# Block-sparse attention into a Sinkhorn mixture of experts: a planned end at the last adding DMA, a later planned landing of the first values, and a new table of priorities

## The chip, the cores and the metric

The kernel runs on one core of one Trainium2 chip. The metric is the time of one execution in device microseconds (us). TensorE (PE) multiplies, VectorE (DVE) and ScalarE (ACT) read its results out of PSUM and work elementwise, GpSimd (POOL) and SyncE (SP) mostly issue DMAs, as ScalarE does now and then. Each of these engines takes its own instructions strictly in the order in which the program holds them: an instruction that waits holds up all that stand behind it on its engine.

## The reference

q, k and v have the shape (4, 8, 768, 64): 4 batches, 8 heads, 768 positions. Attention looks at a band of near positions and at 24 block summaries (the maximum of the keys, the mean of the values of 32 positions each):

```python
k_sum = k.reshape(B, H, nb, block, D).max(axis=3)        # block = 32
v_sum = v.reshape(B, H, nb, block, D).mean(axis=3)
mask_l = np.abs(pos[:, None] - pos[None, :]) < window    # window = 16
scores_all = np.concatenate([scores_l_m, scores_s], axis=-1)   # scores_s has + log(32)
...                                                      # softmax -> a
attn = np.matmul(a, np.concatenate([v, v_sum], axis=2))
```

Its result, as x of 3072 rows and 512 columns, goes through 8 experts, whose weights per row come from 8 Sinkhorn steps:

```python
P = np.exp(x @ w_gate - max)                 # 3072 x 8
for _ in range(8):
    P /= P.sum(1, keepdims=True) + 1e-09
    P /= P.sum(0, keepdims=True) + 1e-09
    P *= N / E
for e in range(E):
    out += P[:, e:e + 1] * (np.maximum(x @ w1[e], 0.0) @ w2[e])   # w1[e]: 512 x 1024, w2[e]: 1024 x 512
```

## The kernel before, in words

**The planner.** The order of the instructions is made when the program is built, by the class `Plan` (lines 39 to 130), a list scheduler. The kernel hands it units: each has an engine (or a choice between two) with a planned cost in us, units that it depends on, a priority (the smaller number first), PSUM banks that it opens or uses, and a `lag`, the planned time from its end until those that depend on it may start. `order()` lays the units out in planned time, and the functions of the units are called in that order, which thereby becomes the order of each engine's queue. At each step it takes, engine by engine, the unit that can start first; among those that can start within 0.02 us of each other the priority decides. A unit without a function (`fn` is None) issues nothing. Such units stand on names that are no engines, `"LAND"` above all: they only tell the plan when a transfer has landed. The waits that the hardware performs come from what the instructions read and write, not from the plan. Where the plan sees TensorE idle during the first stage, `plan.idle` puts in filler matmuls on zeros (line 597).

**The attention stage.** The 32 heads go in 16 pairs (`i`), four to a batch. GpSimd issues the loads of q, k and v, which also convert the type. For each pair TensorE transposes k and q (`tkq`), ScalarE or VectorE copies them out as kT and qT, TensorE makes the scores of the band (`sg`) and of the summaries (`ss`), ScalarE the exponentials, and TensorE multiplies with the values. `block_sums(i)` (line 398) are six matmuls that sum the values of each block (`vs`); they read v as loaded (`vx`) and depend in the plan on the unit `U["v", i]`. `block_out(i)` (from line 402) scales them into `V_s` on VectorE. For pair 0, k and q come in through separate loads in halves; `load_pair(0, "v")` puts the load of v into the plan and sets `U["v", 0]` to its landing. The pairs of batch 0 are worked on in halves of 384 rows, and expert 0 (`hidden0`, `hps` at line 226; `project0`, `yps` at line 236) runs between the pairs as soon as its rows of x are there. For the later batches `near_values` brings the neighbours' values in place through SyncE's queue, and some of k is transposed by DMA (`kT<-kst`).

**Experts 1 to 7.** Each product is a Strassen-Winograd scheme. The rows go in 3 blocks `j` (`NJ`), each in 2 halves `u`: 42 half blocks (`duos`). `plan_duo` plans the first product of one (line 991: `pab`, `pg`; and 1049, 1377), whose results ScalarE copies (`c`, line 1115) and VectorE joins (line 941), with the relu at line 217; VectorE forms the sums of the left-hand sides (`hf`, line 935). `plan_pair` plans the second product of four quarters `c` of each block as seven products `q1` to `q7` (lines 997 and 1377: `px`, `py`); `plan_twin` has one more level for most blocks. For experts from 2 on, ScalarE and VectorE scale the results by P into parts in `out_acc` (`e0` to `e4`: lines 1265, 1246), and GpSimd adds them to `out` in HBM by accumulating DMAs, `da` (line 1286) and `db` (line 1289). `da` needs `e0` and `e3`, and `e3` reads the product `q3`. In the plan the two cost GpSimd 1.0 us each, and the unit `d["landed"]`, which comes 4.0 us later, tells that they have landed.

The last block (expert 7, `j` = 2) goes another way: SyncE fetches the rows as summed so far from HBM (`fetch`), VectorE adds the last products to them (`t0` to `t4`, lines 1231 and 1246), and plain stores (line 1238) on SyncE's queue, two on ScalarE's, write the final rows. So the last adding DMAs are those of the block before it (expert 7, `j` = 1), and no unit of the plan depends on their landing.

**Priorities.** `feed(n)` plans half block n: its first product together with the second product of half block n - 2. `base` is 10000 + 100 n, and each unit's priority is `base` plus a number out of the table `PR` (by `rank`: one for the name, one more for the name in its block), or in the last block one number `name.l<c>` for each quarter:

```python
def rank(name, k):
    return PR[name] + PR.get(f"{name}.{k}", 0.0)
```

The numbers run to several thousand, so they reach far beyond the 100 by which one half block follows the other.

Of the kernel before, what the change touches and what calls it, by code (L numbers as in the profile page):

```python
# [140 lines left out]
def kernel(  # L141
# [12 lines left out]
    B, H, S, D = q.shape  # L154
    G = S // 128
    N, DM = out.shape
    E = moe_w_gate.shape[1]
# [85 lines left out]
    NS = 1  # L243
# [9 lines left out]
    if True:  # L253
# [19 lines left out]
        add = plan.add  # L273
# [574 lines left out]
        load_pair(0, "v")  # L848
        load_pair(1, "k0")
# [70 lines left out]
    if True:  # L920
# [639 lines left out]
        for u in course:  # L1560
# [266 lines left out]
        def feed(n):  # L1827
# [47 lines left out]
            if n < len(duos):  # L1875
# [3 lines left out]
                if e >= 2 and (n == 8 or e > 2 and (j, u) == (0, 0)):  # L1879
                    w2_sub_sums(e, base + PR["NW"], [pairs[1, NJ - 1, 3]["landed"]] if n == 8 else [])  # L1880
# [49 lines left out]
```

## Time and profile before

| | |
|---|---|
| median of 3 runs | 665.35 us (665.2 to 665.42) |
| the profiled execution | 667.84 us |
| its span, first to last instruction | 665.8 us |
| mean granted TensorE clock | 0.993 of full |
| HBM read, written | 55.59 MB, 45.09 MB |

The span is what the trace covers; the time of the execution also holds what lies around it. The second part of the page cuts the span into 40 slices of 16.6 us: each digit is the busy share in tenths (9 is 90% or more), PEclk the granted TensorE clock in tenths of full speed. The fifth groups the instructions: line, engine, operation, output and input, number; then busy time, mean ns of one, and the idle time in front of them with what ended most of it.

```profile
PE   8999999999999999999999999999999999999994
DVE  6879898678899979896799779868888788977874
ACT  5776766555996678898898999988999888998861
POOL 8699504222102022434244243524352436533321
PEclk8999999999999999999999999999999999999998
...
L1286 POOL DMA_DIRECT2D out_dram<-out_acc x68 | 63.9, 940 | 87.4 <-ACT out_acc L1265 47.4
...
L1115 ACT COPY c<-pab 128x512 f32<-128x512 f32 x84 | 50.1, 597 | 15.8 <-PE pab L991 11.5
```

The slices show where TensorE isn't full: the first and the last one. GpSimd issues 68 adding DMAs at line 1286, each of which occupies it for some 0.94 us. The copies at line 1115, one kind of ScalarE's work in the expert stage, take 0.6 us each.

In the views of waits, `<-` names what ended a wait. In a timeline a row begins with its start and its length in us, both for the run of instructions that `x` counts; a number in square brackets is the wait just ahead. The rows that name an engine with a q (SPq, POOLq, ACTq) are the engines' own queue work: DMA issues, semaphores and drains.

### The profile page before, as it was taken

The numbers are of one execution on the slowest core, as the hardware profiler recorded it, in microseconds if no ns is written. First come the engines' busy times: TensorE is split into PE (matmuls) and PEld (weight loads), VectorE is DVE, ScalarE is ACT, GpSimd is POOL, SyncE is SP. The second block draws the span as 40 slices with busy tenths as digits, with TensorE's granted clock in tenths as the row PEclk, the third lists the DMA queues.
The fourth block names the chain that finished last, engine by engine and source line by source line (L and its number), as shares of the span: only waits on it lengthen the run. The fifth ranks groups of instructions, "written<-read, shape, count | busy, mean of one in ns | idle before, by whom it ended". The sixth has DMA issues, their size and how long they took to land.

```text
span 665.8 us, 15109 instructions
## 1 busy us (share of the span) xinstructions
PE 651.5 (98%) x5575; PEld 447.4 (67%) x5575; DVE 545.8 (82%) x1356; ACT 528.7 (79%) x1183; POOL 258.9 (39%) x320
## 2 busy tenths in 40 slices
PE   8999999999999999999999999999999999999994
PEld 4666665555667766676776767767677676776773
DVE  6879898678899979896799779868888788977874
ACT  5776766555996678898898999988999888998861
POOL 8699504222102022434244243524352436533321
PEclk8999999999999999999999999999999999999998
DMA  9999976800727257977989599969997899979576
GB/s 161 184 150 147 132 92 66 103 1 1 142 79 129 96 122 109 115 101 100 170 97 140 69 152 130 110 99 125 139 108 96 115 162 134 148 95 208 88 96 159
DMA packets 147369, 77.75 MB, mean 117 GB/s; under 512 B 112736, under 2 KB 125280, under 8 KB 147296
## 3 DMA queue, kind: packets, MB, share of 16 engines
q0 software_dynamic: 124864, 62.64, 80.7%
q1 hardware_dynamic: 21472, 13.68, 8.3%
q8 instruction: 44, 0.72, 0.4%
q10 hardware_dynamic: 960, 0.48, 0.2%
q14 instruction: 29, 0.24, 0.1%
HBM read 55.59 MB, written 45.09 MB: 151 GB/s over the span
## 4 chain that ended last, share of the span: by engine, by line
PE 82%; DVE 7%; issue 6%; DMA 2%; POOL 2%; POOLq 0%; ACT 0%; DVEq 0%
PE pab L991 16%; PE pg L991 15%; PE py L997 14%; PE px L997 12%; PE px L1377 7%; PE yps L236 5%; PE hps L226 5%; PE pab L1049 4%; DVE xs L552 1%; DMA kT<-kst 1%; DMA vx<-in_v_dram 1%; PE sg L388 1%; POOL out_dram L1289 1%; POOL out_dram L1286 1%; PE tkq L354 1%
## 5 line engine op out<-in xcount | busy, mean ns | idle before, releaser
L997 PEld LDWEIGHTS <-hf 128*128 128x128 f16 x1840 | 179.0, 98 | 50.3
L1289 POOL DMA_DIRECT2D out_dram<-out_acc x68 | 63.8, 938 | 150.9 <-ACT out_acc L1265 88.8
L1286 POOL DMA_DIRECT2D out_dram<-out_acc x68 | 63.9, 940 | 87.4 <-ACT out_acc L1265 47.4
L935 DVE TENSOR_TENSOR hf<-hf 128x1024 f16<-128x1024 f16 x142 | 94.5, 688 | 2.5
L997 PE MATMUL py<-w,hf 128*128 128x256 f16 x656 | 93.8, 273 | 0.0
L941 DVE CUSTOM_DVE_ANT_0 hf<-pg,c 128x512 f16<-128x512 f32 x84 | 57.6, 686 | 30.6 <-ACT c L1115 18.6
L1265 ACT ACTIVATE out_acc<-py,P_sb 128x256 f32<-128x256 f32 x136 | 64.9, 489 | 10.3 <-PE py L997 6.8
L991 PEld LDWEIGHTS <-ws 128*128 128x128 f16 x504 | 47.8, 98 | 30.3 <-issue 0.2
L941 DVE CUSTOM_DVE_ANT_0 hf<-pab,c 128x512 f16<-128x512 f32 x84 | 57.7, 687 | 10.3 <-PE pab L991 4.5
L202 POOL DMA_DIRECT2D w<-in_moe_w_dram x56 | 46.2, 903 | 50.7 <-PE pg L991 44.1
L991 PEld LDWEIGHTS <-w 128*128 128x128 f16 x520 | 48.3, 98 | 24.0 <-issue 0.2
L1115 ACT COPY c<-pab 128x512 f32<-128x512 f32 x84 | 50.1, 597 | 15.8 <-PE pab L991 11.5
L217 ACT ACTIVATE hf<-pg 128x512 f16<-128x512 f32 x84 | 50.4, 601 | 12.0 <-PE pg L991 11.8
L997 PE MATMUL px<-ws,hf 128*128 128x256 f16 x400 | 59.8, 273 | 0.0
L997 PE MATMUL px<-w,hf 128*128 128x256 f16 x400 | 58.5, 273 | 0.0
L991 PE MATMUL pab<-xT,w 128*128 128x512 f16 x184 | 53.9, 379 | 0.0
L1107 ACT COPY pg<-pab 128x512 f32<-128x512 f32 x84 | 49.8, 594 | 3.7 <-PE pab L1049 3.6
L217 ACT ACTIVATE hf<-pab 128x512 f16<-128x512 f32 x84 | 51.1, 615 | 1.5 <-PE pab L991 0.9
L1122 ACT COPY c<-pg 128x512 f32<-128x512 f32 x84 | 49.7, 592 | 1.4 <-PE pg L991 0.8
L991 PE MATMUL pg<-xTs,w 128*128 128x512 f16 x168 | 50.0, 379 | 0.0
L991 PE MATMUL pg<-xTs,ws 128*128 128x512 f16 x168 | 50.0, 379 | 0.0
L991 PE MATMUL pg<-xT,w 128*128 128x512 f16 x168 | 50.0, 379 | 0.0
(190 smaller groups left out, 1513.6 us busy)
## 6 DMA issues: line engine op xcount, KB each, us to landing
out_dram<-out_acc POOLq DMA_DIRECT2D x136, 256.0 KB, 5.2
w<-in_moe_w_dram POOLq DMA_DIRECT2D x8, 1024.0 KB, 11.3
w<-in_moe_w_dram POOLq DMA_DIRECT2D x56, 128.0 KB, 4.9
out_dram<-out_acc SPq DMA_DIRECT2D x28, 256.0 KB, 2.1
vx<-in_v_dram POOLq DMA_DIRECT2D x16, 192.0 KB, 6.0
qst<-in_q_dram POOLq DMA_DIRECT2D x31, 96.0 KB, 5.5
kst<-in_k_dram POOLq DMA_DIRECT2D x24, 96.0 KB, 5.2
out_acc<-out_dram SPq DMA_DIRECT2D x8, 256.0 KB, 5.0
```

Of the source, the lines that this page charges most:

```text
L217: nc.scalar.activation(out=out, in_=in_, func=AF.Relu, bias=0.0, scale=1.0)
L935: nc.vector.tensor_tensor(out=out, in0=in0, in1=in1, op=ALU.subtract)
L941: nc.vector._custom_dve(TENSOR_ADD_SAT, out=out, in0=in0, in1=in1, s0=FLT_MAX, s1=0.0)
L991: nc.tensor.matmul(bank[:], lhsT=w[:, dk, :], rhs=x[:, dk, :], start=start and dk == 0, stop=dk == KH - 1, skip_group_check=True)
L997: nc.tensor.matmul(bank, lhsT=a(f)[:, 128 * c:128 * (c + 1)], rhs=w[:, f, :], start=start and f == 0, stop=f == FH - 1, skip_group_check=True)
L1107: nc.scalar.copy(out=B["g" + K][:], in_=B["a" + K][:])
L1115: nc.scalar.copy(out=B["c5" + K][:], in_=B["b" + K][:])
L1122: nc.scalar.copy(out=B["c2" + K][:], in_=B["g" + K][:])
L1265: nc.scalar.activation(out=out_acc[:, (c, HT + c)[t == tb], k * DH:(k + 1) * DH], in_=at(src), func=AF.Copy, scale=scale[:, t, e:e + 1])
L1286: nc.gpsimd.dma_start(out=rows(ta), in_=out_acc[:, c, :], accum_op=ALU.add)
L1289: nc.gpsimd.dma_start(out=rows(tb), in_=out_acc[:, HT + c, :], accum_op=ALU.add)
L1377: nc.tensor.matmul(half(b, k)[:, g, :], lhsT=still2(e, j, g, w, c)[:, i, :], rhs=moving2a(e, g, v)[:, i, :], start=start and g == 0 and i ...
```

## The change

Three edits. First, behind the load of pair 0's values, a unit that issues nothing moves `U["v", 0]` by 1.6 us in the plan; `block_sums(0)` is planned from there:

```diff
         load_pair(0, "v")
+        U["v", 0] = add("LAND", 0, None, [U["v", 0]], lag=1.6)
         load_pair(1, "k0")
```

Second, in `feed`, once the last half block is planned, a unit `END` that issues nothing depends on the landing of the last adding DMAs:

```diff
+            if n == len(duos) + 1:
+                put("END", 0, None, [pairs[E - 1, NJ - 2, c]["landed"] for c in range(4)], 0)
             m = n - 2
```

Third, the numbers of the table `PR` are replaced; its names stay. A few of them, among them those of the last block's `q3` and `t0` to `t4`:

```diff
         PR = {
-            "m1": 2584.1, "m5": 3374.6, "m2": -1146.9, "m6": -1658.9, "m3": -213.8, "m7": 4417.6,
+            "m1": 2568.5, "m5": 1010.4, "m2": -2957.6, "m6": -785.6, "m3": 391.2, "m7": 2631.7,
...
-            "Nn5": 302.7, "Nnh": -1488.9, "Nn2": 1284.0, "Nn6": -1478.7, "Nj1": -592.1, "Nn3": -840.8,
+            "Nn5": -2485.2, "Nnh": 1513.2, "Nn2": -262.5, "Nn6": -1417.6, "Nj1": 1456.6, "Nn3": -646.5,
...
-            "q7.l2": -1606.8, "q7.l3": -662.9, "q3.l0": 3956.3, "q3.l1": -2000.3, "q3.l2": 6715.0, "q3.l3": 1656.4,
+            "q7.l2": 712.5, "q7.l3": 357.8, "q3.l0": 308.9, "q3.l1": 1053.1, "q3.l2": -1088.2, "q3.l3": 2816.7,
...
-            "t4.l0": 1238.0, "t4.l1": 112.5, "t4.l2": 1173.3, "t4.l3": 1316.2, "t3.l0": -1821.8, "t3.l1": -1533.0,
-            "t3.l2": 74.3, "t3.l3": -1579.2, "ahead.l0": -197.7, "ahead.l1": 265.4, "ahead.l2": -1009.2, "ahead.l3": -449.6,
+            "t4.l0": -148.8, "t4.l1": -1643.2, "t4.l2": -862.2, "t4.l3": 91.1, "t3.l0": 266.6, "t3.l1": 104.4,
+            "t3.l2": -179.6, "t3.l3": -789.1, "ahead.l0": 3599.1, "ahead.l1": -760.6, "ahead.l2": -865.2, "ahead.l3": 1525.2,
```

What the edits do to the queues, as the two built programs show it: the operations are the same, with 24 filler matmuls in each. In the attention stage the order differs only in some 480 instructions at TensorE's start: `vs` of pair 0 stands behind the scores `sg` and the summaries `ss` of pair 0, two fillers and pair 1's transposes, and its `block_out` behind the next copy to qT on VectorE. From the expert stage on, all engines have another order. At the end the `q3` that feeds the last adding DMA is 64 matmuls ahead of TensorE's last one instead of 4, and VectorE's last three are t1, t3, t4 instead of t2, t4, t3. Lines behind 848 stand one further down in the changed kernel, those behind 1880 three.

146 rows, old and new, of the table PR are left out of this document.

## The prediction

> **What bounds the kernel now.** I read the page first, then busy time by stage, then TensorE's waits, then the last ten microseconds engine by engine.
>
> ```profile
> span 665.8 us, 15109 instructions
> PE 651.5 (98%) x5575; PEld 447.4 (67%) x5575; DVE 545.8 (82%) x1356; ACT 528.7 (79%) x1183; POOL 258.9 (39%) x320
> ```
>
> TensorE (PE) is busy for 98% of the span. Where the rest lies is told by windows that I set at the clock's steps and at the ends of the stages:
>
> ```profile
> core 0: us, PE busy (x) PEld busy (x) DVE busy (x) ACT busy (x) POOL busy (x), PEclk, DMA share, GB/s
> 4.78:8.19 3.41, 1.77 (x21) 0.86 (x22) 1.71 (x5) 1.14 (x2) 3.41 (x6) 1.00 1.70 152
> 8.19:11.60 3.41, 3.24 (x35) 2.01 (x35) 1.80 (x8) 1.59 (x3) 3.38 (x5) 0.50 1.54 181
> 11.60:15.02 3.42, 3.36 (x60) 2.24 (x58) 3.17 (x12) 2.15 (x4) 3.31 (x5) 1.00 2.07 159
> 30.00:110.00 80.00, 78.95 (x904) 49.97 (x902) 71.49 (x219) 58.06 (x97) 46.87 (x58) 1.00 1.64 120
> 166.00:650.00 484.00, 484.00 (x3918) 345.44 (x3917) 402.69 (x905) 419.24 (x992) 169.22 (x200) 1.00 0.81 120
> 650.00:656.20 6.20, 6.14 (x56) 5.23 (x54) 5.59 (x15) 1.52 (x4) 0.86 (x1) 1.00 0.68 188
> 656.20:665.80 9.60, 0.00 (x0) 0.00 (x0) 0.77 (x2) 0.47 (x1) 0.86 (x1) 0.71 0.54 124
> ```
>
> From 166 to 650 us, where experts 1 to 7 run and nearly all new numbers act, TensorE is busy for 484.00 of 484.00 us. A new order can win nothing there and can only lose. What can be won is at the two ends: some 1.6 us of waiting and 3.4 us at half clock before 12 us, and 9.6 us after the last matmul.
>
> **The end.** The timeline of the last microseconds, then SyncE's row of the same view:
>
> ```profile
> 654.65 1.54 ACTq L1238 DMA_DIRECT2D out_dram<-out_acc  x2
> 655.11 1.04 PE L997 MATMUL py<-w,hf 128*128 128x256 f16 x8
> 655.32 0.47 DVE L1246 SCALAR_TENSOR_TENSOR out_acc<-pab,nP,out_acc 128x256 f32<-128x256 f32 x1
> 655.71 0.87 DVE L1231 SCALAR_TENSOR_TENSOR out_acc<-pg,P_sb,out_acc 128x256 f32<-128x256 f32 x2
> 656.24 0.47 ACT L1265 ACTIVATE out_acc<-py,P_sb 128x256 f32<-128x256 f32 x1 [2.79 <-DVE out_acc L1231]
> 656.49 0.47 DVE L1231 SCALAR_TENSOR_TENSOR out_acc<-py,P_sb,out_acc 128x256 f32<-128x256 f32 x1
> 657.00 0.86 POOL L1286 DMA_DIRECT2D out_dram<-out_acc  x1 [2.64 <-ACT out_acc L1265]
> ...
> 648.39 9.34 SPq L1238 DMA_DIRECT2D out_dram<-out_acc  x10
> ```
>
> The last matmul ends at 656.15, the last sum of the last block (t3) at 656.96, and SyncE has issued its last store at 657.73. But GpSimd issues one more adding DMA at 657.00: `da` of the block before (e = 7, j = 1), whose q3 stood last but one on TensorE. Two views say how long that lasts, the rows of the program's end (line 1925) and the DMA issues from 645 us on:
>
> ```profile
> L1925 SPq EVENT_SEMAPHORE  x11: 17/28/2857, 657.8 to 665.7; - x11
> L1925 POOLq DRAIN  x3: 44/93/8007, 657.0 to 665.5; - x3
> ...
> out_dram<-out_acc SPq DMA_DIRECT2D x4, 256.0 KB, 2.1
> out_dram<-out_acc SPq DMA_DIRECT2D x6, 128.0 KB, 2.8
> out_dram<-out_acc POOLq DMA_DIRECT2D x2, 256.0 KB, 4.4
> ```
>
> SyncE stands in one wait of 2.86 us for this DMA. GpSimd's drain begins at 657.0 and takes 8.01 us, to 665.0; the rest of the program takes 0.8 us. So the span ends 8.8 us after the issue of the last adding DMA, not after the last store. The Trainium skill ("VectorE: DVE Perf Modes", section "The DRAIN you can't avoid") gives the drains at a program's end about 12 ns each; SyncE's 7 ns agree, GpSimd's 8007 ns do not, and the measurement decides. With a drain of 12 ns the add would cost only its landing, and this edit some 2.5 us less.
>
> In the built programs the last matmul of that q3 stands 4 matmuls ahead of TensorE's last one before, and 64 after. At 6.14 us for 56 matmuls (0.11 us each), it ends 7.0 us ahead of TensorE's end instead of 0.4. ScalarE's copy of it, which now also stands behind the issue of two stores (654.65 to 656.19), then has nothing in front: it starts near 649.3, the add is issued 0.76 us later as in the rows above, near 650.1, and 8.0 us of drain bring it to 658.1. That is ahead of the stores, which set the end next. VectorE's last three are now t1, t3, t4; t4 waits for t1 and stands behind t3, and from the group that ends 3.06 us ahead of the end on they follow each other every 0.39 us (655.32 to 655.71), so the last ends near 657.24, 0.3 later than now, and SyncE's last store starts near 657.4. Landing takes 2.0 us (the 2.1 of stores with no add beside them) to 2.8 (the late ones beside one), so 659.4 to 660.2; SyncE's remaining waits take 0.1 to 0.4 and the end 0.8. The span would end between 660.3 and 661.4 with TensorE where it is: 4.4 to 5.5 us less. I take **-4.9**, the middle, since the moved add no longer lands among the last stores but two stores still go out on ScalarE's queue.
>
> **The start.** TensorE's waits, whole run:
>
> ```profile
> PE vs L398 <- DMA vx<-in_v_dram: 1.6, 1, 1.6
> ...
> PE tx L559 <- DVE xs L552: 0.3, 1, 0.3
> PE vs L398 <- DVE xs L552: 0.3, 1, 0.3
> ```
>
> and the timeline around the first one:
>
> ```profile
> 2.71 0.73 POOL L293 DMA_DIRECT2D kst<-in_k_dram  x1
> ...
> 5.43 0.80 ACT L222 COPY kT<-tkq 128x768 bf16<-128x768 bf16 x1 [0.31 <-PE tkq L351]
> 5.49 1.26 PE L597 MATMUL idle<-zeros 128*128 128x512 bf16 x3
> 5.60 0.56 DVE L222 COPY qT<-tkq 128x384 bf16<-128x384 bf16 x1 [0.88 <-PE tkq L338]
> ...
> 8.36 0.80 PE L398 MATMUL vs<-vx,m_blk 128*128 128x128 bf16 x6 [1.61 <-DMA vx<-in_v_dram]
> 9.10 0.60 PE L388 MATMUL sg<-qT,kT 64*128 64x160 bf16 x8
> ...
> 10.48 0.85 PE L351 MATMUL tkq<-ident,kst 128*64 128x128 bf16 x12
> ...
> 22.93 0.65 PE L226 MATMUL hps<-xT,w 128*128 128x384 f16 x3
> ```
>
> The block sums of pair 0 wait for v, and the scores queue behind them although kT and qT are there at 6.23. The change puts scores, two fillers and the summaries ahead, and pair 1's transposes too, so scores start at 6.75. The next wait is pair 1's k: issued at 2.71 and landing after about 6.2 us (the row below), near 9.0.
>
> ```profile
> kst<-in_k_dram POOLq DMA_DIRECT2D x3, 192.0 KB, 6.2
> ...
> 75.83 0.36 DVE L380 TENSOR_TENSOR kh<-kT 128x384 bf16<-128x384 bf16 x1 [1.02 <-DMA kT<-kst]
> ```
>
> So the transposes move from 10.48 to 9.0 at best, 1.5 us, and the block sums behind them find v. The fillers number 24 in both programs. From there VectorE is the narrow place (3.17 of 3.42 us busy) and now has the 0.3 us of block_out inside its busy stretch, so I expect 0.8 to 1.0 us left when hps begins at 22.93. After that TensorE is dense, and the advance is kept unless a transfer with its own clock takes it: at 75.83 VectorE waited 1.02 us for a transposing DMA, with a relu behind it that TensorE needs. That DMA is queued behind SyncE's near_values, which follow TensorE, so part of it moves along. Bounds: nothing is kept (0), all of the wait is (-1.6). I take **-0.6**.
>
> The clock fell to 0.50 for 3.41 us right behind a stretch of equal length with 1.77 us busy. In the changed kernel that stretch holds 1.2 us more work and the wait for k falls mostly into the next one. The Trainium skill ("TensorE: Matmul & The Clock Gate", section "Part 1: The HAM clock gate") says that a free-running window of about 3.4 us decides on half clock; the steps in the trace agree, though by that page an idle window does it, and here a half-idle one did.
>
> **The middle.** All new PR values change the order alone: the work is the same, but each matmul that reads what ScalarE or VectorE made can now stand closer behind it. In both built programs the shortest distance between a feeding matmul and the one that reads the result is 0.86 us of matmuls, so neither is tighter by itself; what differs is who queues on ScalarE, busy 419 of 484 us. Cost: 0 from below, as now. From above the nearest rows are those between 30 and 110 us, where VectorE is 89% busy and TensorE loses 1.05 of 80 us; over 484 us that is 6.4. I take **+0.3**, near the lower end, since the stage itself shows 0 with queues as full. The END entry has no function to call: it issues nothing and costs 0, and no work is needed to hide it.
>
> **The sum.** -4.9 - 0.6 + 0.3 = -5.2 us on the span, 665.8 to 660.6. The profiled execution took 667.84 us, 2.04 around its span; the median of the three runs shown is 665.35. I take the same 5.2 off the median: **660.2 us**.
>
> **The rivals.**
> *The half clock moves instead of going.* In the changed kernel 8.19 to 11.60 begins with the wait for k and holds perhaps 2.3 us of work, between the 1.77 that was followed by half clock and the 3.24 that was not. If it falls, the work of 11.60 to 15.02 (3.36 us at full clock) runs at half: up to 1.7 us, part of it under VectorE. The start's -0.6 becomes about +0.2: 661.0 us. The Trainium skill's same page (its section on transposes) says that transposes do not count as activity; under that rule this is likelier, since pair 1's transposes lie there.
> *Slower: ScalarE's queue holds TensorE up once in each half block.* There are 42 of them. If in each one in-order ScalarE stands waiting in front of a copy (mean 0.6 us) that TensorE reads next, from 0.13 us each the 5.5 us of the ends are used up; at 0.3 us it is 12.6 us, some 672.8. For it: ScalarE has 13% to spare. Against it: VectorE, not TensorE, does the waiting now, and the distances are equal.
> *Some of it:* 2 to 5 us of such stalls: 662 to 665.
> *The drain does not follow the add* (its 8 us fixed from some other event): only the start is left, 665.0 us.
>
> **How the numbers follow.** Forecast 0.59, moved half clock 0.13, some stalls 0.13, the slower rival 0.10, the drain 0.05. No change is within 0.2%, 664.0 to 666.7. Faster: the first two and most of the third, 0.83; same: the drain and a little, 0.07; slower 0.10. The range leaves out the slower rival, the drain, the worse third of the stalls and a little below: from -4.9 - 1.6 at the best, 658.6, to 3.6 us of stalls more, 663.8.
>
> **What would show it.** GpSimd's last adding DMA about 6 to 7 us ahead of TensorE's end, its drain ended before SyncE's, and 4 to 5.5 us from the last matmul to the end instead of 9.6; no wait of block sums on v, a wait of about 1 us on k near 8 to 9 us, hps near 22, the half clock gone; TensorE's busy share from 166 us on still whole. I am wrong if the drain ends as late as before, or if TensorE shows waits of microseconds between 166 and 650.

## The result, and the profile after

| | before | after |
|---|---|---|
| median | 665.38 us (665.20 to 665.57, 4 runs) | 661.01 us (660.79 to 662.95, 4 runs) |
| ratio | | 0.9941 (95% interval 0.9922 to 0.9960) |
| the profiled execution, its span | 667.84 us, 665.8 us | 661.13 us, 659.1 us |

The change takes 4.37 us off the median. The two profiles are 6.7 us apart in span, because the profiled execution of before was itself 2.5 us over its median, and the profiled one of after is not; this matters below.

The first lines of the page of after: the span, then the engines' busy time.

```profile
span 659.1 us, 15106 instructions
...
PE 650.6 (99%) x5575; PEld 446.3 (68%) x5575; DVE 546.6 (83%) x1356; ACT 528.0 (80%) x1183; POOL 260.2 (39%) x320
```

The windows of after, at the places of those of before and around its own end:

```profile
4.78:8.19 3.41, 2.92 (x32) 1.22 (x32) 2.46 (x10) 2.24 (x4) 3.41 (x6) 1.00 1.62 151
8.19:11.60 3.41, 2.87 (x55) 2.06 (x56) 2.82 (x11) 1.84 (x3) 3.41 (x5) 1.00 1.64 186
11.60:15.02 3.42, 3.42 (x75) 2.56 (x73) 3.28 (x13) 2.25 (x5) 3.42 (x5) 1.00 2.12 167
166.00:645.00 479.00, 478.71 (x3868) 340.45 (x3866) 398.44 (x887) 415.45 (x986) 167.92 (x198) 1.00 0.81 120
655.00:659.10 4.10, 0.00 (x0) 0.00 (x0) 1.00 (x3) 0.00 (x0) 0.00 (x0) 1.00 0.57 196
```

The reader is to see three things. The stretch behind TensorE's last matmul is 4.3 us instead of 9.6. The half clock is gone from 8.19 to 11.60. From 166 to 645 us TensorE is still full to 0.3 us in 479.

The timeline of the end of after, then the rows of the program's end (line 1928: `x`, the shortest, median and longest in ns, first and last start):

```profile
648.66 0.86 POOL L1287 DMA_DIRECT2D out_dram<-out_acc  x1 [2.50 <-ACT out_acc L1266]
648.85 7.61 SPq L1239 DMA_DIRECT2D out_dram<-out_acc  x8
...
654.25 0.60 PE L998 MATMUL pg<-w,hf 128*128 128x256 f16 x4
...
655.52 0.48 DVE L1232 SCALAR_TENSOR_TENSOR out_acc<-py,P_sb,out_acc 128x256 f32<-128x256 f32 x1
```

```profile
L1928 SPq EVENT_SEMAPHORE  x12: 17/28/28, 656.5 to 659.1; - x12
...
L1928 POOLq DRAIN  x3: 44/93/8492, 648.6 to 658.9; - x3
L1928 SPq DRAIN  x3: 7/7/7, 658.3 to 658.6; - x3
```

The last adding DMA goes out at 648.66, 6.2 us ahead of the last matmul's end (654.85) instead of 0.85 us behind it. GpSimd's drain is as long as before (8.49 us), but begins at 648.6 and is over at 657.1, before SyncE's at 658.3. SyncE's one long wait of 2.86 us is gone: its longest is 28 ns. What sets the end now is the landing of the last plain store.

### The profile page after: what moved, and what is told of

It is laid out like the page before. It is cut to its first block, busy times and chain, and to the rows that moved or that the text cites. A ratio compares the mean times of both kernels' runs of the same rounds, so it can differ in the third digit from the quotient of the medians.

```text
span 659.1 us, 15106 instructions
## 1 busy us (share of the span) xinstructions
PE 650.6 (99%) x5575; PEld 446.3 (68%) x5575; DVE 546.6 (83%) x1356; ACT 528.0 (80%) x1183; POOL 260.2 (39%) x320
## 4 chain that ended last, share of the span: by engine, by line
PE 86%; DVE 7%; DMA 3%; issue 1%; POOL 1%; ACT 0%; DVEq 0%; POOLq 0%
PE pab L992 16%; PE pg L992 16%; PE py L998 16%; PE px L998 13%; PE px L1378 7%; PE yps L236 5%; PE hps L226 5%; PE pab L1050 4%; DVE xs L552 1%; DMA kT<-kst 1%; DMA w<-in_moe_w_dram 1%; DMA kst<-in_k_dram 1%; PE sg L388 1%; PE tkq L354 1%; DVE em L440 1%
## 5 line engine op out<-in xcount | busy, mean ns | idle before, releaser
L202 POOL DMA_DIRECT2D w<-in_moe_w_dram x56 | 44.6, 844 | 49.1 <-PE pg L992 46.8
L992 PE MATMUL pab<-xT,ws 128*128 128x512 f16 x168 | 50.0, 379 | 0.0
```

Source lines behind the costliest of these rows:

```text
L992: nc.tensor.matmul(bank[:], lhsT=w[:, dk, :], rhs=x[:, dk, :], start=start and dk == 0, stop=dk == KH - 1, skip_group_check=True)
```

## The experiments

All were compared with the kernel before on the same chip. The table reads every profile at the same three places: the start of the last two matmuls into `sink` (of the last of the eight Sinkhorn steps, line 1517 or 1518; expert 0's matmuls still run there), the end of the last matmul, and the end of the span. The middle is the time from the first of these to the second, the tail from the second to the third.

| kernel | ratio to before (95%) | sink at, us | middle | tail | span |
|---|---|---|---|---|---|
| before (the first profile) | | 162.56 | 493.6 | 9.6 | 665.8 |
| base (before again) | 1.0001 (0.9992 to 1.0010) | 159.85 | 495.4 | 9.4 | 664.7 |
| start_only | 0.9999 (0.9991 to 1.0008) | 159.68 | 495.0 | 9.6 | 664.3 |
| order_only | 0.9934 (0.9922 to 0.9947) | 160.12 | 494.6 | 4.1 | 658.9 |
| after | 0.9941 (0.9922 to 0.9960) | 160.00 | 494.9 | 4.3 | 659.1 |
| after_again | 0.9939 (0.9925 to 0.9952) | 160.38 | 495.1 | 4.1 | 659.6 |
| late_add | 1.0007 (0.9997 to 1.0017) | 159.74 | 495.8 | 9.1 | 664.6 |
| early_add | 0.9984 (0.9973 to 0.9996) | 160.59 | 497.2 | 5.4 | 663.1 |
| q3_only | 0.9950 (0.9936 to 0.9964) | 160.31 | 494.7 | 5.4 | 660.4 |
| two_products | 0.9932 (0.9920 to 0.9945) | 160.43 | 494.4 | 4.2 | 659.0 |
| two_products_start | 0.9939 (0.9927 to 0.9951) | 160.15 | 494.7 | 4.2 | 659.1 |
| gp_store | one run | 160.00 | 495.8 | 7.5 | 663.3 |
| pool_op | one run | 159.79 | 495.0 | 6.4 | 661.2 |
| later_w1 | 1.0355 (1.0336 to 1.0374) | 160.16 | 521.0 | 5.3 | 686.4 |

The `END` entry by itself was not run: with it alone the built program holds the same instructions in the same order as before, so it wins nothing by itself.

### base: was the profiled execution like the others?

No edit.

> The kernel before, unchanged, profiled anew: the profiled execution of before took 667.84 us, the others 665.2 to 665.6, while the profiled one of after (661.13) is like the others of its kernel. Theory: the 3.4 us at half clock belong to that one execution, not to the kernel; then the other executions have a span near 663.4, a clock of 1.00 throughout, and the change could not win them. Rival: the half clock is in every execution of before (clock 0.993, a window of 0.50 near 8 to 12 us), and the 2.5 us lie elsewhere.

Its first stretch, then TensorE's waits:

```profile
4.78:8.19 3.41, 3.21 (x37) 2.03 (x37) 2.06 (x8) 1.44 (x3) 3.41 (x6) 1.00 1.71 156
8.19:11.60 3.41, 3.10 (x56) 2.20 (x55) 3.09 (x13) 2.20 (x4) 3.41 (x5) 1.00 1.54 185
```

```profile
PE pg L991 <- DVE hf L941: 1.6, 1, 1.6
...
PE idle L597 <- ACT Es L483: 0.3, 1, 0.3
```

No half clock at the start, and no wait on v: a wait of 1.6 us, on which the prediction built its start, was in one execution alone. In the five other profiles with the old start it is 0 to 0.65 us. The DMA issues say why: the first load of v in the profile of before, then in base (the last number is us from issue to landing):

```profile
vx<-in_v_dram POOLq DMA_DIRECT2D x1, 192.0 KB, 6.8
```

```profile
vx<-in_v_dram POOLq DMA_DIRECT2D x1, 192.0 KB, 5.2
```

Base has another wait instead, of 1.6 us in the middle, whose chain its timeline shows:

```profile
289.59 0.29 DVE L938 TENSOR_TENSOR ws<-w 128x256 f16<-128x256 f16 x1 [1.87 <-DMA w<-in_moe_w_dram]
...
291.40 0.59 PE L991 MATMUL pg<-xTs,w 128*128 128x512 f16 x2 [1.62 <-DVE hf L941]
```

VectorE stands in front of a sum over a weight that has not landed (its two loads were issued at 281.1 and 281.8), and the join that TensorE needs stands behind it. Base's two loads, then order_only's, which had no such wait:

```profile
w<-in_moe_w_dram POOLq DMA_DIRECT2D x2, 128.0 KB, 7.1
```

```profile
w<-in_moe_w_dram POOLq DMA_DIRECT2D x2, 128.0 KB, 5.4
```

This wait comes and goes with the landing, up to 1.6 us under the old order and up to 0.5 us under the new: it belongs to neither. The expected span of 663.4 without the half clock was right but for this.

### start_only and order_only: the two halves of the change

The start alone, in the kernel before, and everything but the start:

```diff
         load_pair(0, "v")
+        U["v", 0] = add("LAND", 0, None, [U["v", 0]], lag=1.6)
```

```diff
 (the changed kernel)
         load_pair(0, "v")
-        U["v", 0] = add("LAND", 0, None, [U["v", 0]], lag=1.6)
```

> Only the 1.6 us of planned landing of v are added to the kernel before. Theory: the order of the first 12 us alone wins 0.2 to 0.8 us (ratio 0.9988 to 0.9997), since part of the wait on v comes back as a wait on pair 1's k, and more only where half clock is in the ordinary executions of before. Rival: the start won its full 1.6 us and more (ratio 0.9975 or less). Rival: nothing is kept, ratio 1.000.

> The new priorities and END without the landing of v. Theory: the tail's gain of 5.4 us (9.6 to 4.2 from the last matmul to the end) less some 1.2 us of new small waits in the middle: 661.2, ratio 0.9937, with the wait of 1.6 us on v back. Rival: the start gave a third of the gain or more: ratio 0.996 or above.

The new priorities give the whole gain: 0.9934. The start gives nothing that can be measured: 0.9999, nearest to the rival that nothing is kept, and its interval leaves out a gain of 0.1% (0.6 us) or more. In the profiles the last `sink` stands at 159.68 to 160.38 with it (eight, mean 159.99) and at 159.85 to 160.59 without (five but the first profile, mean 160.26). If it wins 0.3 us, that is less than the spread. The rival that all of the 1.6 us were to be won falls. The expected wait of 1.6 us on v did not come back in order_only either: v landed after 5.5 us there, and nothing waited for it. The profile of start_only shows what waits with the changed start:

```profile
PE pg L992 <- DVE hf L942: 0.7, 1, 0.7
PE tx L559 <- DVE xs L552: 0.7, 2, 0.4
PE tkq L351 <- DMA kst<-in_k_dram: 0.3, 1, 0.3
```

Pair 1's k now keeps TensorE waiting, and VectorE does at `tx` (twice, where before had it once). The first row is the late weight of the section above.

### late_add: the last adding DMA put back

The changed kernel with one product late:

```diff
 (the changed kernel, in plan_pair)
+                              + (10000.0 if (e, j) == (E - 1, NJ - 2) and name in ("q3",) and c == 3 else 0.0),
```

> The changed kernel with one product alone put late: q3 of quarter 3 of the block (7, 1) stands last on TensorE, so the last adding DMA is issued after the last stores. Theory: GpSimd's drain ends 8 us after that issue (issue near 656, drain to 664, end near 664.8): 5 to 6.5 us slower than after, 666 to 668 us, slower than before. Rival: the add costs only its own landing (about 5 us from issue, end near 662): 3 us slower than after. Rival: the add doesn't set the end and the gain came from the order in general: within 0.5 us of after.

```profile
656.30 0.86 POOL L1287 DMA_DIRECT2D out_dram<-out_acc  x1 [9.49 <-ACT out_acc L1266]
```

```profile
L1929 SPq EVENT_SEMAPHORE  x11: 17/28/3254, 656.7 to 664.5; - x11
L1929 POOLq DRAIN  x3: 40/102/7435, 656.3 to 664.2; - x3
```

The first view is the last row of its timeline, the second its program's end. TensorE's order is that of the changed kernel but for its last 68 matmuls. The one DMA costs the whole gain: 1.0007, the tail 9.1 us, SyncE's long wait back (3.25 us). The last adding DMA is the cause; the rival that the order in general did it falls, and so does the one that the add costs only its own landing: the add landed at 660.6, and the span ended at 664.6.

### early_add, two_products, q3_only: the same from the other side

If that DMA is the cause, moving its products forward in the kernel before should do without the new table. Three edits of the same line of `plan_pair`, in the kernel before:

```diff
 early_add
+                              + (-10000.0 if (e, j) == (E - 1, NJ - 2) and name in ("q2", "q4", "q7", "q3") else 0.0),
 two_products
+                              + (-10000.0 if (e, j, c) == (E - 1, NJ - 2, 3) and name in ("q7", "q3") else 0.0),
 q3_only
+                              + (-1000.0 if (e, j, c) == (E - 1, NJ - 2, 3) and name == "q3" else 0.0),
```

> The kernel before with one thing put early: the products q2, q4, q7 and q3 of the block (7, 1) go first among what is ready, so the last adding DMA's products end 9 us ahead of TensorE's end instead of 0.4; only some 500 of TensorE's last rows stand otherwise. Theory: this alone brings the end from 9.4 us behind the last matmul to 4.2 to 4.6 us: 4.8 to 5.4 us less, ratio 0.992 to 0.993, as much as the whole change or a little more, since the middle keeps the old order. Rival: the gain lies in the new order as a whole, then this wins less than 2.5 us (ratio above 0.996).

early_add won 1.1 us instead of 5. Its tail is 5.4 us, a us more than foreseen, but TensorE's last 30 us are not whole any more: the middle is 497.2. Its waits from 620 us on:

```profile
PE px L997 <- DVE py L938: 1.0, 2, 0.6
PE py L997 <- DVE py L938: 0.6, 1, 0.6
```

With all sixteen products moved, TensorE waits for the sums that VectorE makes of the products (`py`, line 938). Its stores suffered too. The DMA issues of early_add from 650 us on, then of after from 645 us on:

```profile
out_dram<-out_acc SPq DMA_DIRECT2D x5, 128.0 KB, 4.0
```

```profile
out_dram<-out_acc SPq DMA_DIRECT2D x6, 128.0 KB, 2.2
```

The stores of 128 KB took nearly twice as long to land, beside three adding DMAs that went out between 648.5 and 650; whether these were the reason was not tested. So early_add could not settle the question, and I made the edit smaller.

> The kernel before, but of the products of the block (7, 1) only q7 and q3 of quarter 3 are put early (early_add moved q2, q4, q7 and q3 of all four quarters, and TensorE then waited 2.6 us in its last 30 us for VectorE and ScalarE). The last adding DMA's products now end 11.8 us ahead of TensorE's end, and no result is read sooner behind its feeding matmul than before; some 150 of TensorE's last rows stand otherwise. Theory: no new waits in the last 30 us and an end 4.2 to 4.8 us behind the last matmul instead of 9.4, so 4.6 to 5.2 us less than before, ratio 0.992 to 0.993, as fast as the changed kernel or up to 1 us faster. Rival: early_add's small gain was no accident of its waits: the gain needs the whole new order, and this wins 1 to 2 us (0.997 to 0.9985).

> two_products with the 1.6 us of planned landing of v besides. Theory: as start_only showed none, the start adds nothing: within 0.4 us of two_products. Rival: it wins 0.5 us or more on the executions in which v lands late.

> The changed kernel, unchanged, on the same chip as the two others. Theory: 4 to 4.5 us under the kernel before (ratio 0.9930 to 0.9942), 0 to 1 us slower than two_products, since its new order has some 1 us more of small waits between 166 and 645 us. Rival: it is the faster of the two by 0.5 us or more.

Two of the sixteen products are enough. The rows of two_products: GpSimd's last two adding DMAs, then the program's end:

```profile
643.54 0.86 POOL L1286 DMA_DIRECT2D out_dram<-out_acc  x1 [1.30 <-ACT out_acc L1265]
644.08 1.21 POOL L1289 DMA_DIRECT2D out_dram<-out_acc  x1
```

```profile
L1926 POOLq DRAIN  x3: 44/93/8842, 644.0 to 658.7; - x3
L1926 SPq DRAIN  x3: 7/7/7, 658.2 to 658.5; - x3
```

With the old table, it issues the last adding DMA 10.7 us ahead of the last matmul's end (654.81), has a tail of 4.2 us and a ratio of 0.9932, as fast as the changed kernel (0.9939) within the intervals: 4.35 us off the median, a little short of the 4.6 to 5.2 expected. That it is the faster of the two, as expected, can't be told: the medians on that chip are 661.57 and 661.52. The start added nothing to it either (0.9939). No version here beats the changed kernel beyond doubt.

> The kernel before with q3 alone of quarter 3 of the block (7, 1) put early, by 1000 in its priority. The last adding DMA is then db, whose last product (q7) ends 3.9 us ahead of TensorE's end. Theory (the drain ends 3.15 us after that DMA has landed, the span 0.8 us after the drain): ScalarE and VectorE take 1.2 to 1.5 us, so the issue comes some 2.6 us ahead of the last matmul's end, the landing 4.3 to 4.8 us later, the drain to 4.9 to 5.3, the end 5.6 to 6.1 us behind the last matmul, between the 9.4 of before and the 4.2 of two_products: 3.3 to 3.8 us under before, ratio 0.9943 to 0.995. Rival: SyncE's stores already set the end there, 4.2 to 4.5 us behind the last matmul, as fast as two_products.

```profile
652.35 0.86 POOL L1289 DMA_DIRECT2D out_dram<-out_acc  x1 [6.64 <-DVE out_acc L1270]
```

```profile
L1926 POOLq DRAIN  x3: 40/102/7297, 652.3 to 660.1; - x3
L1926 SPq DRAIN  x3: 7/7/13, 659.1 to 659.9; - x3
```

The point between: the add goes out 2.7 us ahead of the last matmul's end (655.04), the drain ends at 659.6, just behind SyncE's store waits at 659.1, and the tail is 5.4 us. Its add took 4.1 us to land and the drain 3.15 more; the stores were done 4.1 us behind the last matmul here and 3.4 in after. The gain is 3.2 us on the median, just under the 3.3 to 3.8 expected. An issue 10.7 us ahead (two_products) wins no more tail than one 6.2 us ahead (after). Where the limit lies was not tried; my estimate is 4 to 5 us, since single adds took 7.3 to 8.5 us from issue to the drain's end and SyncE's stores were done 3.4 us behind the last matmul.

### gp_store and pool_op: what GpSimd's drain waits for

The changed kernel, with its very last store on GpSimd's queue instead of SyncE's, and with one GpSimd copy of a single element behind the last sum:

```diff
 gp_store
-                    "sb0": stores(tb, (0, 1), nc.sync), "sb1": stores(tb, (1, 2), nc.scalar), "sb": stores(tb, (0, 2), nc.sync)}
+                    "sb0": stores(tb, (0, 1), nc.gpsimd if c == 2 else nc.sync), "sb1": stores(tb, (1, 2), nc.scalar), "sb": stores(tb, (0, 2), nc.sync)}
 pool_op
+                if c == 2:
+                    put("POOL", 0.1, lambda: nc.gpsimd.tensor_copy(out=warm[0:1, 0:1], in_=out_acc[0:1, LAST_B[2], 0:1]), [d["t4"]], prio)
```

> The changed kernel, but its very last store (128 KB, a plain one) goes out on GpSimd's queue instead of SyncE's. In six profiles GpSimd's drain ended 3.15 us after the last adding DMA had landed. Theory: it does so for any DMA of GpSimd: issued near 656.1, landed near 658.5 to 660.5, drain to 661.7 to 663.7, the span ends 0.8 us later, 3 to 5 us after the changed kernel's 659.1. Rival: only adding DMAs hold the drain: within 1 us of 659.1.

> The changed kernel with one GpSimd copy of a single element more, which waits for the last sum on VectorE (it writes a tile that nothing reads). Theory: the drain follows GpSimd's DMAs, so behind a late instruction without a DMA it takes well under 1 us and the span stays at 659.1, within 0.7. Rival: the drain takes its 8 us behind GpSimd's last instruction whatever that is: the drain ends near 664, span near 665.

gp_store: its last row of GpSimd's timeline, the landing of that DMA, the drain; then pool_op's last row of GpSimd's timeline, and its drain:

```profile
657.21 0.57 POOL L1239 DMA_DIRECT2D out_dram<-out_acc  x1 [6.77 <-DVE out_acc L1232]
```

```profile
out_dram<-out_acc POOLq DMA_DIRECT2D x1, 128.0 KB, 2.0
```

```profile
L1928 POOLq DRAIN  x3: 46/102/5223, 657.2 to 662.9; - x3
```

```profile
656.03 0.18 POOL L1792 COPY warm<-out_acc 1x1 f32<-1x1 f32 x1 [6.53 <-DVE out_acc L1232]
```

```profile
L1930 POOLq DRAIN  x3: 40/102/4380, 656.0 to 660.9; - x3
```

The plain store holds the drain as the adding DMA does: issued at 657.2, landed 2.0 us later, drained at 662.4, 3.2 us after the landing. The span is 4.1 us longer than after's, 3.2 us of it in the tail and 0.9 in the middle, though TensorE's order is the same. pool_op surprised me: with nothing but a copy of 0.18 us behind the last sum (656.03) the drain took 4.38 us and ended at 660.4, and the span was 661.2, 2.1 us longer. GpSimd's own last DMA had landed at 653.65, SyncE's last store at 657.8; what the drain waited for is open. So neither reading was right as I had put it: a late GpSimd instruction without a DMA doesn't cost the 8 us, but it isn't nearly free either. Each of the two is one run.

### later_w1: chasing the wait for the weights

```diff
 (the changed kernel, with early_add's line)
             load(("w1", e, i), lambda: load_w1(e, i), 0.85, 3.5, deps)
+            U["w1", e, i] = add("LAND", 0, None, [U["w1", e, i]], lag=2.5)
```

> The changed kernel with the products of the last adding DMAs put early as in early_add, and with 2.5 us more of planned landing for the first weights of experts 1 to 7 (planned 4.7 us after the issue, 5.4 to 7.7 us in five profiles, after which VectorE, and TensorE behind it, waited up to 1.6 us near 290 us). Theory: these waits go, 0.3 to 1.5 us less than after (660 or less, ratio 0.990 to 0.993), and the times of single executions lie closer together. Rival: the new order that comes with it brings as many small waits of its own: within 1 us of after, or slower.

24 us slower. The waits that it was to remove are replaced by many others, the largest groups of which are:

```profile
PE pab L1050 <- DVE pab L939: 3.6, 6, 1.0
PE px L1378 <- DVE px L939: 1.9, 4, 0.8
PE pab L992 <- ACT pg L1108: 1.8, 5, 0.6
```

A likely reason, not tested: another planned time lets other units meet in the planner's windows of 0.02 us, and the table's numbers then decide between pairs for which they were not made. Whether a table made for these times would win the 0 to 1.6 us was not tried. early_add's line, which is in it too, can account for little of the loss: in the kernel before it changes TensorE's order only from matmul 5322 of 5575 on, and that matmul already starts 23.9 us later here (649.66) than in after (625.76).

## Why the prediction was right, point by point

**The end: right, and a little better than -4.9.** Tails of 9.4 to 9.6 us became 4.1 to 4.3, so -5.3. The add went out 6.2 us ahead of the last matmul's end, against 6.0 in the forecast (650.1 against 656.15). The stores, now alone, landed at the fast end of the range given (2.2 us median, the last ones 2.0). The rival that the drain has another cause fell with late_add.

**The drain: right in its effect, wrong in its form.** I took 8.0 us from the issue as a fixed length. It was 8.0 by accident. Of the twelve profiles in which GpSimd's last work is an adding DMA, eleven have a drain of 7.3 to 10.6 us that ended 3.15 us after that DMA had landed: before 4.83 us to landing and 3.15 more, after 5.32 and 3.15, early_add 7.29 and 3.15. The landings of the last adding DMA in before and in after:

```profile
out_dram<-out_acc POOLq DMA_DIRECT2D x1, 256.0 KB, 4.8
```

```profile
out_dram<-out_acc POOLq DMA_DIRECT2D x1, 256.0 KB, 5.3
```

In the twelfth, later_w1, it ended 0.4 us after the landing; why is open. The forecast stood because the drain ended a microsecond ahead of the stores by either reading. The Trainium skill's page "VectorE: DVE Perf Modes" ("The DRAIN you can't avoid") gives a program's last drains some 12 ns; SyncE's 7 to 13 ns agree in every profile, GpSimd's long one in none, and TensorE, VectorE and ScalarE have one of 0.15 to 1.6 us each.

**The start: mis-sized, -0.6 against 0 to -0.3.** This is the step that failed. The rows were read rightly, the scores went ahead and the wait on k came as foreseen, as the row from the waits of after shows:

```profile
PE tkq L351 <- DMA kst<-in_k_dram: 0.9, 1, 0.9
```

But a wait on v as long as 1.6 us and the 3.4 us at half clock were in that one execution alone (the other profiles with the old start wait 0 to 0.65 us on v): its last `sink` stood at 162.56, those of all thirteen others at 159.7 to 160.6. The prediction had both numbers in hand, 667.84 for the execution and 665.35 for the median, and took all 5.2 us off the median without asking where the 2.5 us lay. They lay in the stretch from which it took the start's gain.

**The half clock: neither removed nor moved.** No other profile has it at the start. The section of the Trainium skill's page "TensorE: Matmul & The Clock Gate" that the prediction named ("Part 1: The HAM clock gate") fits in so far: the stretch ahead of it was 1.77 of 3.41 us busy in the execution that had it, and 2.56 to 3.22 in the thirteen others. No run here tells from which share on it falls.

**The middle: mis-sized, +0.3 against up to +0.8.** Less the waits that VectorE hands on from late weights, the middle takes 493.6 us in before, 493.8 in base and 494.3 in start_only, and 494.6 to 494.9 in order_only, after and after_again. But q3_only and two_products, with the old table, stand at 494.0 and 494.4, and the medians show no such price: two_products and after_again, with nearly the same tail, take 661.57 and 661.52. What lengthens the middle is not shown: TensorE's gaps add up to 0.2 to 0.5 us in the three new ones. That a new order "can win nothing there" held for the one execution that the prediction read; base waits 1.6 us in that stretch. All of it is far from the slower rival's 5.5 us.

**The sum.** From the profiles, -5.3, about -0.2 and +0.8 make -4.7, against -4.37 measured on the median and -5.2 forecast: the tail was 0.4 better, the start and the middle together 0.9 worse, and 0.3 is left over, less than executions of one kernel differ by (660.79 to 662.95). But two_products, with the old order in the middle, wins no more (-4.35) with the same tail. So what takes some 0.9 us of the tail's gain away is not shown to be the new order. 661.01 lies in the range, 0.8 above the forecast. That it is also the 661.0 of the rival in which the half clock moves is chance: after and the other profiles have full clock there. One slip of the working: by its own terms the lower end of the range is 665.35 - 6.5 = 658.85, not 658.6.

## What to carry to other kernels

At the end of a program ask each engine when its drain can end, not only which store lands last: here GpSimd's drain mostly ended 3.15 us after its last DMA had landed, so its last work belongs well ahead of the end, and the late stores on another queue. A new table of hundreds of priorities can owe its gain to the place of two products; test by moving the one suspect late in the new kernel and early in the old one, in as small an edit as will do it. And before a term of a sum is taken from a single profile, set that execution's time against the median: if it is an outlier, find out in which stage before predicting to remove it.

## What the runs showed of the hardware that I had not expected

- GpSimd's drain at the program's end lasted to 3.15 us after its last adding DMA had landed in eleven profiles of twelve (0.4 us in the other), 3.2 us behind a plain store of 128 KB, and 4.2 us behind a copy of one element, 6.7 us after GpSimd's own last DMA had landed.
- The landing of GpSimd's converting loads varies from one profile to the next: the first v of 192 KB in 5.2 to 6.8 us, the weights of 128 KB issued near 281 us in 5.1 to 7.7 us. In a tuned order this shows as waits of 0 to 1.6 us on TensorE, two engines away.
- The half clock for 3.4 us near the start was in one of fourteen profiles, behind the stretch with the least TensorE work (1.77 of 3.41 us).
